# Moving chunk 1's transposes of x from TensorE to the DMA, with a new sequence of turns, in a gated linear attention and MLP kernel

## Chip, cores and metric

One core of one Trainium2 chip runs the whole kernel in one launch. The metric is the device time in microseconds (us) of the execution, median of several runs.

## What is computed

The input is q, k, v and alpha of 4 batches, 8 heads, 768 steps and 48 channels a head. The attention part is a recurrence, and a normalised two-layer MLP with a residual follows it. The reference, cut to what matters:

```python
for t in range(S):
    state = alpha[:, :, t, :, None] * state + einsum('bhd,bhe->bhde', k[:, :, t], v[:, :, t])
    y[:, :, t] = einsum('bhd,bhde->bhe', q[:, :, t], state)
x = y.transpose(0, 2, 1, 3).reshape(B, S, H * D)              # 4 x 768 x 384
mu, var = mean(x), mean((x - mu) ** 2)                        # over the 384 channels
xn = (x - mu) / sqrt(var + 1e-06) * g_ln
out = x + maximum(xn @ w_ch1, 0.0) @ w_ch2                    # 384 -> 1536 -> 384
```

The MLP's weights arrive as 64-bit floating-point words and are turned into 32-bit ones on the chip.

## The kernel before

The 768 steps are cut into six chunks of 128. For each chunk and batch (24 pairs) a generator `attention(c, b)` takes the logarithm of alpha (L285), sums it along the chunk with a triangular matrix on TensorE (L290 for chunk 0, L501 later), scales q and k with its exponentials (L295, L296, L304), turns them (for chunks 0 and 1 with TensorE, L320, and copies to qT and kT, L325 and L327; later through DRAM with a transposing transfer, L335 to L342), forms the scores `aps` (L354, L517), the state's update `ups` (L384) and the output `yps` (L408 for chunk 0, L424 later). ScalarE and VectorE then evict x with its sum (L438 to L445), write it out for the residual (L452), compute the variance (L459 to L462) and the normalised xn (L465 or L469).

The MLP needs x with channels on the partitions. There are two ways for that. For chunks below `X_BY_DMA`, TensorE transposes three 128x128 blocks of xn for each batch (L476), and VectorE copies the result into `xT` (L479 for chunk 0, L482 for others). For the later chunks, xn is split into the two 16-bit halves of each word (`parts`, L485), written to DRAM (`sentx`, L488) and read back with a transposing transfer (L490). The engine of the copy at L485 follows from `PARTED`: GpSimd for chunks below it, ScalarE from it on.

```python
def part(c):
    return nc.gpsimd.tensor_copy if c < PARTED else nc.scalar.copy
...
if c < X_BY_DMA:
    xps = ps.tile([P, NF, P], FP32, name="xps", tag="bank", bufs=8)
    ...
else:
    parts = work.tile([P, 2, DM], UINT16, name="parts", tag="row", bufs=ROWS)
    part(c)(out=parts, in_=xn.bitcast(UINT16).rearrange("t (d w) -> t w d", w=2))
    ...
    nc.sync.dma_start(sent, parts)
    ...
    nc.sync.dma_start_transpose(xT_of[c][:, :, b].bitcast(UINT16),
                                sent.rearrange("t w d -> (t w) d"))
```

The weights come in twelve pieces, named A to L in the sequence, first and second layer in turn. Each is loaded (L191), rounded on VectorE and ScalarE (L201 to L212), and later split into a top and a low part (L226 to L232). The hidden products `hps` (L603) come in groups of 128 hidden channels. For chunk 0 the first ten groups of hidden channels are plain: three products against xT, for two batches at a time where the channel group is one of the first six, else for four. All other groups are "halved": nine products of top, mixed and low parts of weights and x (x split at L554 on ScalarE and L557 on VectorE). The hidden values are evicted as `htop` (L615, ScalarE), `hlow` (L623) and `hmixed` (L632, VectorE); the second layer `ops` (L645) accumulates 384 output channels for each batch, and L664 and L665 add x and store.

Every engine works through its own queue in order, and all transfers but one small one are issued from SP's queue. What stands in these queues, and in which order, is set by the string `ORDER`: each of its characters names a generator (0, 1, 2 the loads of alpha, k and q; 3 those of v; a to x the 24 attention pairs; A to L the weight pieces; M the hidden products, R, N and V their evictions, Y the second layer, X the split of x, Q the results, and so on), and the kernel advances that generator by one step.

```python
with tc.manual_schedule():
    for turn in ORDER:
        next(turns[turn], None)
```

Of the kernel before, what the change touches and what calls it, by code (L numbers as in the profile page):

```python
# [17 lines left out]

EPS = 1e-6
BY_DMA = 2  # L20
X_BY_DMA = 2
STAGED = 3
ROWS = 8
SUMS = 19
# [1 line left out]
TAIL = 3  # L26
KEPT = 2
SPLIT = 6
PARTED = 2
PLAIN = 10  # L30
ROUND_BY_POOL = False
K = 4096.0

ORDER = (
    "000aabc210b21aaaab0dc221b1Aabaadbbbefbaca3acdBc4bddccbcbdcdddAfcaaAbAaAa1eBaaba2"
    "eb3fdCbfabfbBdfbbc0ceBfeeeedf1gdb2BaChCcBcCdd5c34dCMdegMeddMhcgdghhRRRgcg3gfEfhA"
    "cMehfeRec0ChcfeEfhgc5efeeeEYEdgfYeXDgf3fBjfM2RMMhMhFgDD1iRADR4FFRihEYjF3YDhXYjFD"
    "DYFjjXhgjiHMghRjhhhihi0iHigYGYHXYgjgMMgIiAjGkGGijRYRYiHXHXIX1XIIBlMMRR5jKGff43Yl"
    "flkiMKej0KK2R3h0MhKMJIRC1XRKjjejCkFYknjliJ1fUehY2llgJJj0jhehmjkfjgjgkhGYfLi4kiMU"
    "2LLmkmil0lMLRNgLRVjgLgYlTlYYTXXNkiYkXXVXXXiUi3YIUi35onXQXMUplkkQklQlkmRNMiQln0kk"  # L40
    "VlkiiT34knkl2kllRlnnMT1lmONUVRYEjiJN0nYYYmVYETYkpUpMMnnUmmpmlmRGNVk2noIYURNjjkjY"
    "VYYMHHTRll5NV2jmYMnUipniRU13kNpUYnVnqYlYM3iokJnl1pRlnNYmVYo1nTMMUnronooRNRVYYM0N"
    "Vn2UlUUpkRMTYpY4ooUNVXOnXoRNVmYpX0mXUqnnqmmXXmXmXX33mY5npYqorpY3mQqoqqQpoMOrprMs"
    "ORtorNRMVo0qprrNroQropoMoUppRQpRppYYVYYpNYrqq1NVVYM5nY1qmYrRqpqmmNqUp4VYttU2YtM0"
    "qt1pRNUrMoRmOooVNptUUtuYYqoq2YqqMRnnqUoVNVYmsro2Yt3sssssYMRmsMRrUUqqNrVNYYvrqrrr"
    "MMposs1XUVrXrtRNVRYNXXYYXXtVXXXq3YYOY5Qsss4tvMqQvvO0ruuOR2UsUNvQtMsrRtNssssvsuuu"
    "VM0VrtUY1uRssNY3YusrVYYUUvu1YssMvMvQR3qtNRVrYNYtvwxtVttMRYtYu4sNUxUUU5YtVUYuwvrv"
    "vtt22ttwxUMxRutwtNUMVRNYvYYxxvxU3VYMwwxMRNxwYOxVRNVwYYYXMwXMRXNwYXRVNYYVXXXYuOQu"
    "Xvv5XuvwxwwwMRxxx3wuwuNwVMRNuVwOxYYYYUUvwQuuuuMwwvMQRNVRvvvNYMVYYYuOOxRUuNVUYxxY"
    "MxxxRNMYVwUYRwxUvNYQVYxMMRwxxvRONVNYVYYYXXXXXUUMRMUUUNYRXVNVYUMRYNXXYVYYXMQUOMRR"  # L50
    "NYVYNVYYQMRNMYRVYNVYYUUMMRUNVYYRONVMRUNQVOYOOOUYYUYUUMRNMRYMMRNNVVVMRRNVYYYQNVYY"
    "YYQQQQ"
)


# [1 line left out]
def kernel(  # L57
# [212 lines left out]
    def part(c):  # L270
        return nc.gpsimd.tensor_copy if c < PARTED else nc.scalar.copy

# [3 lines left out]
    def attention(c, b):  # L276
# [194 lines left out]
        if c not in xT_of:  # L471
            xT_of[c] = work.tile([P, NF, B, P], FP32, name="xT", tag="xT", bufs=1)
        if c < X_BY_DMA:
            xps = ps.tile([P, NF, P], FP32, name="xps", tag="bank", bufs=8)
# [231 lines left out]
```

## Time and profile before

| | |
|---|---|
| median of 3 runs | 412.56 us (411.27 to 415.81) |
| the profiled execution | 412.15 us |
| its span, first to last instruction | 410.4 us |
| granted TensorE clock, mean | 0.996 |
| busy: TensorE, VectorE, ScalarE, GpSimd | 399.1, 258.3, 221.1, 112.4 us |
| moved by DMA | 66.81 MB |

In the profile, PE is TensorE's products and PEld its loading of weights, DVE is VectorE, ACT is ScalarE, POOL is GpSimd and SPq is SP's queue, which issues transfers. A row of the timeline has the start and the length in us, engine, line, operation, output and inputs, and in square brackets the idle time ahead of it with what ended it. A row of the chain has start, length and the work that the end of the program hangs on there.

### The profile page before, as it was taken

To read this page: it belongs to the slowest core of one execution; us is meant where nothing else is said; L and a number is where in the kernel's file an instruction comes from. 1 tells how busy PE (TensorE), PEld (TensorE's weight loads), DVE (VectorE), ACT (ScalarE), POOL (GpSimd) and SP (SyncE) were. 2 spreads that over 40 slices of the span, in tenths; PEclk is the share of its full clock that TensorE was granted. 3 is DMA by queue.
4 is the path that set the end of the run, shared out by engine and by line. 5 is a ranking of instruction groups with operands and counts; after the bars stand their busy time and mean duration, and the time that the engine had idled before them with its cause. 6 is when DMAs were issued, how large, how long until landed. Compare 5 with 4: busy or idle time off the path is not lost.

```text
span 410.4 us, 10816 instructions
## 1 busy us (share of the span) xinstructions
PE 399.1 (97%) x4418; PEld 334.9 (82%) x4418; DVE 258.3 (63%) x424; ACT 221.1 (54%) x489; POOL 112.4 (27%) x122
## 2 busy tenths in 40 slices
PE   8779999999999999999999999999999999999996
PEld 6668777646789888889888879879989889889886
DVE  4699898989987755775444774463573346443262
ACT  5688687479749674563675648355328443111120
POOL 4224301002145435121243325351041084130000
PEclk9989999999999999999999999999999999999999
DMA  6985996994848769968367958867435032010302
GB/s 193 308 260 150 276 282 193 276 279 159 191 117 256 200 162 207 207 167 247 87 176 193 218 151 250 176 142 195 107 61 173 23 102 53 21 58 2 96 19 77
DMA packets 103562, 66.81 MB, mean 163 GB/s; under 512 B 70444, under 2 KB 95532, under 8 KB 103512
## 3 DMA queue, kind: packets, MB, share of 16 engines
q1 hardware_dynamic: 103480, 66.12, 59.5%
q8 instruction: 34, 0.56, 0.6%
q14 instruction: 16, 0.13, 0.1%
q0 software_dynamic: 32, 0.00, 0.0%
HBM read 34.29 MB, written 20.28 MB: 133 GB/s over the span
## 4 chain that ended last, share of the span: by engine, by line
PE 92%; DMA 3%; ACT 2%; SPq 1%; DVE 1%; issue 1%; ACTq 0%
PE hps L603 39%; PE ops L645 39%; PE yps L424 5%; PE ups L384 3%; PE aps L517 3%; DMA vn<-in_v_dram 2%; PE lps L501 2%; DMA ra<-in_alpha_dram 1%; PE yps L408 1%; PE tps L320 1%; SPq L125 1%; PE xps L476 1%; DVE hmixed L632 1%; ACT xn L459 0%; SPq L129 0%
## 5 line engine op out<-in xcount | busy, mean ns | idle before, releaser
L615 ACT ACTIVATE htop<-hps 128x512 fp32r<-128x512 f32 (+2 forms) x78 | 43.9, 564 | 120.3 <-PE hps L603 116.3
L623 DVE SCALAR_TENSOR_TENSOR hlow<-hps,htop 128x512 fp32r<-128x512 f32 x62 | 42.8, 690 | 90.9 <-ACT htop L615 88.3
L569 POOL TENSOR_TENSOR wmixed<-top,low 128x384 fp32r<-128x384 f32 x62 | 70.1, 1140 | 96.1 <-PE hps L603 41.0
L645 PE MATMUL ops<-top,htop 128*128 128x384 f32 x248 | 56.7, 344 | 0.0
L645 PE MATMUL ops<-low,hmixed 128*128 128x384 f32 x248 | 55.3, 339 | 0.0
L603 PE MATMUL hps<-xtop,top 128*128 128x512 f32 x186 | 54.5, 401 | 0.0
L603 PE MATMUL hps<-xmixed,low 128*128 128x512 f32 x186 | 53.4, 395 | 0.0
L645 PE MATMUL ops<-ws,hlow 128*128 128x384 f32 x240 | 53.4, 338 | 0.0
L603 PE MATMUL hps<-xlow,wmixed 128*128 128x512 f32 x186 | 53.4, 395 | 0.0
L632 DVE SCALAR_TENSOR_TENSOR hmixed<-hlow,htop 128x512 fp32r<-128x512 f32 x62 | 48.0, 779 | 3.2
L645 PEld LDWEIGHTS ops<-top,htop 128*128 128x128 f32 x248 | 44.1, 188 | 3.7 <-ACT xn L469 0.6
L645 PEld LDWEIGHTS ops<-low,hmixed 128*128 128x128 f32 x248 | 44.3, 188 | 0.8 <-DVE hmixed L632 0.3
L645 PEld LDWEIGHTS ops<-ws,hlow 128*128 128x128 f32 x240 | 43.0, 188 | 0.0
L603 PEld LDWEIGHTS hps<-xmixed,low 128*128 128x128 f32 x186 | 35.0, 188 | 8.4
L603 PEld LDWEIGHTS hps<-xlow,wmixed 128*128 128x128 f32 x186 | 34.9, 188 | 8.2
L603 PEld LDWEIGHTS hps<-xtop,top 128*128 128x128 f32 x186 | 33.6, 188 | 6.7 <-DVE mid L392 0.6
L394 POOL TENSOR_TENSOR mid<-mid,gate 112x192 f32<-112x192 f32 x20 | 13.4, 672 | 86.5 <-DVE mid L392 51.9
L335 ACT COPY planes<-qk 128x1024 uint16<-128x1024 uint16 x32 | 32.7, 1039 | 1.5 <-DVE qk L304 1.5
L394 POOL TENSOR_TENSOR st<-st,gate 112x192 f32<-112x192 f32 x16 | 16.1, 1005 | 53.5 <-DVE st L392 51.1
L645 PE MATMUL ops<-w,htop 128*128 128x384 f32 x80 | 27.8, 493 | 0.0
L603 PE MATMUL hps<-xT,w 128*128 128x256 f32 (+1 forms) x96 | 27.1, 433 | 0.0
L603 PEld LDWEIGHTS hps<-xT,w 128*128 128x128 f32 x96 | 18.1, 190 | 8.3 <-issue 5.1
(121 smaller groups left out, 662.2 us busy)
## 6 DMA issues: line engine op xcount, KB each, us to landing
ws<-in_moe_w_ch_dram SPq DMA_DIRECT2D x12, 768.0 KB
sent<-planes SPq DMA_DIRECT2D x32, 256.0 KB
vn<-in_v_dram SPq DMA_DIRECT2D x12, 384.0 KB
kept<-x SPq DMA_DIRECT2D x20, 192.0 KB
rq<-in_q_dram SPq DMA_DIRECT2D x16, 192.0 KB
rk<-in_k_dram SPq DMA_DIRECT2D x16, 192.0 KB
ob<-kept SPq DMA_DIRECT2D x16, 192.0 KB
sentx<-parts SPq DMA_DIRECT2D x16, 192.0 KB
```

The lines of the kernel that those rows point to most:

```text
L335: part(c)(out=planes, in_=natural.rearrange("t (d w) -> t w d", w=2))
L384: nc.tensor.matmul(up[h, p], qk_of(c, b)[1][ts, p, i, :h.stop - h.start], vn[ts, i, p], start=True, stop=True)
L394: nc.gpsimd.tensor_mul(new, new, gate[:R, s].unsqueeze(2).broadcast_to([R, NP, D]))
L424: nc.tensor.matmul(yps[r][halves[s], i, p], of, by, start=not (odd and inner), stop=bool(inner or not odd), skip_group_check=bool(odd))
L501: nc.tensor.matmul(lps[halves[h ^ i ^ 1], :DM], tri[halves[h], halves[h]], las[c, b + i][halves[h]], start=True, stop=True)
L517: nc.tensor.matmul(aps[halves[i ^ n], p, s], kT[rs, p, s], qT[rs, p, s], start=True, stop=True)
L569: nc.gpsimd.tensor_add(mixed_of[g], *(first_weights(w, g[1]).bitcast(FP32) for w in (top_of, low_of)))
L603: nc.tensor.matmul(hps, ws[n][:, f], xs[f][n][:, cs], start=(n == f == 0), stop=(n == len(ws) - 1 and f == NF - 1))
L615: nc.scalar.activation(out=t, in_=hps, func=AFT.Relu, scale=1.0 if g in halved else K ** -2)
L623: nc.vector.scalar_tensor_tensor(out=t, in0=hps, scalar=0.0, in1=top.bitcast(FP32), op0=AOP.max, op1=AOP.subtract)
L632: nc.vector.scalar_tensor_tensor(out=t, in0=low.bitcast(FP32), scalar=1 - K, in1=top.bitcast(FP32), op0=AOP.mult, op1=AOP.add)
L645: nc.tensor.matmul(acc_of[c, b], hidden_of[g][n + 1][:, (b - bs[0]) * P:][:, :P], by, start=(j == n == 0), stop=last)
```

## The change

`X_BY_DMA` goes from 2 to 1, so chunk 1's x takes the way of the split halves and the transposing transfer; only chunk 0 is still transposed on TensorE. `PARTED` goes from 2 to 1; with both, the copy at L485 of chunk 1 is ScalarE's. `ORDER` is replaced by another string; both are cut here to their first three lines and the last.

```diff
 BY_DMA = 2
-X_BY_DMA = 2
+X_BY_DMA = 1
 STAGED = 3
...
-PARTED = 2
+PARTED = 1
...
 ORDER = (
-    "000aabc210b21aaaab0dc221b1Aabaadbbbefbaca3acdBc4bddccbcbdcdddAfcaaAbAaAa1eBaaba2"
-    "eb3fdCbfabfbBdfbbc0ceBfeeeedf1gdb2BaChCcBcCdd5c34dCMdegMeddMhcgdghhRRRgcg3gfEfhA"
-    "cMehfeRec0ChcfeEfhgc5efeeeEYEdgfYeXDgf3fBjfM2RMMhMhFgDD1iRADR4FFRihEYjF3YDhXYjFD"
...
-    "YYQQQQ"
+    "000aa2bbcca12130ba2aacbaabbbAbaaaadab1cbbbbAc1adbc2abdc0a0Babaabdcda1bbdAdcedda2"
+    "fAbhbcgdA44deCBM3ffecRfBMfRBffcedegCefeec3BC1dc5hdC2dCdge3heeBcddhceMdRMccgffhhd"
+    "RhhAfcgfAgdge0gfCEEce5eghYEYiefEe1cgf3CEjMRDfM2FDRfFDfDM3RMMXFg4iejFYYgRiFgYYefh"
...
+    "NVYYYQQQYQ"
 )
```

More of the change, by code (lines that the diff above doesn't have):

```diff
@@ L34 @@
 ORDER = (
-    "000aabc210b21aaaab0dc221b1Aabaadbbbefbaca3acdBc4bddccbcbdcdddAfcaaAbAaAa1eBaaba2"
-    "eb3fdCbfabfbBdfbbc0ceBfeeeedf1gdb2BaChCcBcCdd5c34dCMdegMeddMhcgdghhRRRgcg3gfEfhA"
-    "cMehfeRec0ChcfeEfhgc5efeeeEYEdgfYeXDgf3fBjfM2RMMhMhFgDD1iRADR4FFRihEYjF3YDhXYjFD"
-    "DYFjjXhgjiHMghRjhhhihi0iHigYGYHXYgjgMMgIiAjGkGGijRYRYiHXHXIX1XIIBlMMRR5jKGff43Yl"
-    "flkiMKej0KK2R3h0MhKMJIRC1XRKjjejCkFYknjliJ1fUehY2llgJJj0jhehmjkfjgjgkhGYfLi4kiMU"
-    "2LLmkmil0lMLRNgLRVjgLgYlTlYYTXXNkiYkXXVXXXiUi3YIUi35onXQXMUplkkQklQlkmRNMiQln0kk"
@@ L41 @@
[L41 to L51, printed above, removed]
-    "YYQQQQ"
+    "000aa2bbcca12130ba2aacbaabbbAbaaaadab1cbbbbAc1adbc2abdc0a0Babaabdcda1bbdAdcedda2"
@@ new lines @@
+    "fAbhbcgdA44deCBM3ffecRfBMfRBffcedegCefeec3BC1dc5hdC2dCdge3heeBcddhceMdRMccgffhhd"
+    "RhhAfcgfAgdge0gfCEEce5eghYEYiefEe1cgf3CEjMRDfM2FDRfFDfDM3RMMXFg4iejFYYgRiFgYYefh"
+    "hHjjRhXffgYhYgHgjgefDgiI0iYHEHGHXMMR1RiXkGXXGiiYYjlMGhhKRhjYhghjGj4IKMMXCh3KRIeY"
+    "lKEIRhXKlJhhYXMMigjgIgKJieJJgRf52RLUe3fjMjhilhLFLgejfYjUGLA0lYRlkUkhlMk0NjLjLTkl"
+    "kkYTVXiXkXjllkXjjkYRi1NVYiXmjiYXXU3QiinXiUiB4XDQ5nm1MBTUkRk3MQlljjljNROmkj22lknM"
+    "kkVlN0IQ3kiniUVlknkYnRnDiNnYTkmUG0mmH2iYYVMYYmRNYijF3VYnpl3ol4jJlMllHmTMRlNRYnVN"
@@ new lines @@
+    "lp1mV3lYYIJ2k0TYlUmoMppkRj115NUVYY0mnnnUinlopppnoMmoRNnViUnTrnpYqnk0YopoUkmo1MpR"
+    "mnkNVoMmYoRmUUYmm2kmN4V5q0lpYrYqoToornOXprM2XrR3sXqMNVo1omq2RNYXqrr1YYorXVXXq3Xr"
+    "oXqYotUonop4QUpstrq2MUnRNQOqMppto3ppVnppoRN3MtYoYYpVYo0nUQMmUmRmRmnONVNYUvQo1YY5"
+    "ttMqrVrrnoYrRUMtspstUNRVsN1YrppVYYYsttMrspqRsNY0rrrrq0qMpVRuqqYsqqqsOO2UmN425Vss"
+    "YtmuuvYsvuMMUspuu3uRRvU0tuNYVNVYYY2Xv1MvMvXXRN2VXXXRwUUNsYUVUvqvXYYYqqqtXXqvMuRQ"
+    "QtttutNMVO1xttRtstQ4sNss5vvutuxu33vxMUrvRwYYYVttxNVxUYMwxrRrNVYsOsY3YYMRxMqNVYRY"
@@ L53 @@
+    "tUtNVssutUUUMrrRNVwwvwYrxYQssYwwYMMRNVquYYsURNYxVYuuvvrXXuwwMXUMRNVRYNMvYUxVXXXX"
+    "RYYONXO5XxUVvvxxvwwxwwxYMRNYQwxxQwxwvYwxwUUOVYwMRvwMRxNVNVUuuuYwYYYUMMRNRVNVYYYY"
+    "MxwUxRNwUMUUVYYvvxURNYOuVYQxMMuOURRxNYVUNYUYVYMMuXXXRNVYYRMNXXXVYXXRNVYXYYQMOQMR"
+    "RNVNYYVYQYOQUUMMORONYVRYNUVMRNYVYYYUUMRNMVRNVOOYQYYYUUUUUMMRNRYMVMMNVRYYYORRNVNV"
+    "NVYYYQQQYQ"
 )
```

## The prediction

> **What bounds the kernel now.** I read the page's first parts, then the busy time by stage, then the chain that ended last in order of time.
>
> ```profile
> span 410.4 us, 10816 instructions
> PE 399.1 (97%) x4418; PEld 334.9 (82%) x4418; DVE 258.3 (63%) x424; ACT 221.1 (54%) x489; POOL 112.4 (27%) x122
> ...
> GB/s 193 308 260 150 276 282 193 276 279 159 191 117 256 200 162 207 207 167 247 87 176 193 218 151 250 176 142 195 107 61 173 23 102 53 21 58 2 96 19 77
> ```
>
> ```profile
> 0.00:20.00 20.00, 15.79 (x138) 12.07 (x139) 10.93 (x31) 12.14 (x26) 6.75 (x18) 0.99 0.78 248
> 20.00:40.00 20.00, 17.73 (x307) 15.47 (x304) 18.18 (x32) 17.36 (x47) 6.75 (x6) 0.93 0.71 215
> 40.00:60.00 20.00, 19.41 (x387) 15.37 (x386) 18.14 (x32) 15.03 (x36) 4.02 (x5) 1.00 0.93 267
> 80.00:100.00 20.00, 20.00 (x185) 11.06 (x174) 18.41 (x30) 17.11 (x41) 3.57 (x4) 1.00 0.76 241
> 240.00:280.00 40.00, 39.23 (x415) 33.23 (x414) 22.02 (x38) 24.51 (x54) 16.48 (x16) 1.00 0.74 179
> 360.00:410.40 50.40, 46.95 (x238) 42.53 (x236) 19.00 (x30) 6.59 (x11) 3.92 (x3) 1.00 0.14 49
> ```
>
> The columns after the length are PE, PEld, DVE, ACT and POOL busy, then granted clock, DMA share and GB/s. TensorE bounds the kernel: 11.3 us of it are idle, of which the first 60 us hold 7.1 (4.21, 2.27 and 0.59), the stage from 240 holds 0.77, and the end 3.45. VectorE is the second engine: above 18 us of 20 in the three later early stages shown. So a change can gain at the start, where TensorE has holes, or by taking work off TensorE; later only the order's small losses are left.
>
> The first 35 us are worse than the busy column says. On the chain and among TensorE's and VectorE's instructions:
>
> ```profile
> 11.37 7.47 DMA vn<-in_v_dram
> ...
> 34.91 4.08 PE hps L603 x18
> ...
> 47.84 2.78 PE ops L645 x8
> 50.61 5.18 PE hps L603 x24
> ```
>
> ```profile
> 7.83 0.56 DVE L304 TENSOR_TENSOR qk<-rq,eq 128x384 f32<-128x384 f32 x1 [0.28 <-DMA rq<-in_q_dram]
> ...
> 8.97 0.69 DVE L325 COPY kT<-tps 112x512 f32<-112x512 f32 x1
> ...
> 17.72 0.56 DVE L201 TENSOR_SCALAR w<-ws 128x768 int32<-128x768 int32 x1 [1.04 <-DMA ws<-in_moe_w_ch_dram]
> ...
> 20.94 0.96 DVE L209 SCALAR_TENSOR_TENSOR ws<-ws 128x768 int32<-128x768 int32 x1 [0.80 <-ACT ws L207]
> ...
> 35.63 0.94 DVE L212 TENSOR_TENSOR w<-w,ws 128x768 f32<-128x768 f32 x1
> ...
> 46.31 1.15 DVE L212 TENSOR_TENSOR w<-w,ws 128x768 f32<-128x768 f32 x1
> ```
>
> The steady stream of hidden products (hps, L603) starts at 34.9 us. Ahead of it TensorE waits for v, then for the chain of statistics behind v, while VectorE rounds weights (L201 to L212). The first weight piece (letter A) waits for its transfer until 17.72; the second hidden piece (C) is rounded by 36.57, and the third (E) by 47.46. The stream of four plain groups at 50.61 uses E.
>
> **The change, part by part.**
>
> *Transposes taken off.* Twelve of the 24 transposes at L476 go (three for each batch of chunk 1), and the four copies at L482.
>
> ```profile
> 82.51 7.72 PE hps L603 x18
> ...
> 94.69 0.48 PE xps L476 x3
> 97.75 0.66 PE xps L476 x6
> 106.65 0.33 PE xps L476 x3
> ```
>
> ```profile
> L482 DVE COPY xT<-xps x4: 551/553/559, 97.2 to 107.7; 128x384 f32<-128x384 f32 x4
> L485 ACT COPY parts<-xn x16: 815/828/834, 138.9 to 332.6; 128x768 uint16<-128x768 uint16 x16
> L488 SPq DMA_DIRECT2D sentx<-parts x16: 332/400/607, 140.5 to 334.9; - x16
> L490 SPq DMA_TRANSPOSE xT<-sentx x16: 1215/1252/1565, 143.2 to 338.4; - x16
> ```
>
> On the chain the twelve cost 0.48 + 0.66 + 0.33 = 1.47 us, and TensorE is what the chain runs through there: minus 1.5. VectorE loses 4 x 0.55 = 2.2 us, in the stage where it is fullest; I count that at nothing by itself, since it only keeps VectorE from catching up with TensorE.
>
> *Added.* Four copies on ScalarE (4 x 0.83 = 3.3 us), four writes and four transposing transfers on SP's queue (4 x 0.40 + 4 x 1.25 = 6.6 us of issue). PARTED falls with X_BY_DMA, so the copy of chunk 1 is ScalarE's, as it was for chunks 2 to 5. All this I cost at nothing if the cover holds: ScalarE is busy 17.11 of 20 in the stage from 80, so 2.9 us stand free there, and more in front of it. For the transfers the cover is the TensorE work between the first such copy and the first product of chunk 1. The built order has there one run of six plain 512-wide products, eight plain second-layer ones, two halved groups of nine, 24 second-layer products, and attention: by counts and the chain's rows (7.72/18 = 0.43 us a pass of a plain one, two passes each, and below 2.1 for nine or twelve of the others) about 25 us. What must fit is bounded by chunk 2 of today: first copy at 138.9, last transpose issued at 159.72.
>
> ```profile
> 159.72 1.25 SPq L490 DMA_TRANSPOSE xT<-sentx  x1
> ...
> 166.46 0.71 ACT L554 ACTIVATE xtop<-xT,small 128x512 fp32r<-128x512 f32 x1
> 168.02 0.60 ACT L615 ACTIVATE htop<-hps 128x512 fp32r<-128x512 f32 x1 [0.84 <-PE hps L603]
> ```
>
> That is 22 us to the last issue, or 27.6 to the first use, with the four copies spread over 12 us by the order; the new order has them within seven instructions of ScalarE, so I estimate 16 to 20 us and a free margin of 5.
>
> The Trainium skill, page "VectorE: DVE Perf Modes", section "Rules for kernel authors", speaks against the change: it sends a 128x128 transpose to TensorE where PSUM can take it and to the DMA only otherwise, and its section "The three transpose paths" gives, for one of 16-bit elements, 390 ns against 1309. The rows here agree in size (0.11 to 0.16 us for one on the chain, 1.25 us to issue three), but the dearer path is paid on another engine; by the rule alone the four batches would cost some 5 us instead of saving 1.5.
>
> *The new sequence at the start.* v of batches 0 and 1 moves from the 18th issue on SP's queue to the 8th, weight piece A from the 17th to the 13th. Today the seventh load (196.6 KB each, so 1.38 MB) has landed at 7.83 by the L304 row; v adds 0.39 MB, at the 193 to 308 GB/s of the first two slices 1.3 to 2.0 us: v lands near 9.4 instead of 18.84. It then no longer bounds; TensorE's wait for it goes. Piece A now stands behind two small writes that wait for ScalarE's exponentials, whose ends today let it go near 7.65 (estimate):
>
> ```profile
> 6.80 0.48 ACT L295 ACTIVATE eq<-lps 128x384 f32<-128x384 f32 x1
> ...
> 10.89 0.43 SPq L191 DMA_DIRECT2D ws<-in_moe_w_ch_dram  x1
> ```
>
> Issued at 10.89 it was used at 17.72, 6.83 us later; the same again gives 14.5, so VectorE starts on A 3.2 us earlier. But three L304 (0.56) and two kT copies (0.69) that stood ahead of A now stand behind it; started every 0.47 and 0.6 us they are about 2.7 us, and by E's end the built order has 3.9 us more there. So C is rounded by 36.57 - 3.2 + 2.7 = 36.1, less what VectorE saves of its waits on the way (today 17.9 us between these ends hold 15.6 us of instructions, and 0.80 of the rest is the wait shown): 33.8 to 36.1. E: 47.46 - 3.2 + 3.9 = 48.2, less 0 to 4.1 (29.7 us that hold 25.6): 44.1 to 48.2. The third plain group starts today about 37.6 (two groups of six passes into the run of 18), a microsecond after C; in the new order it can only start with C, so 1.5 to 3.8 us earlier. From there to the run at 50.61 the new order has about 0.5 us less TensorE work, so that run comes 2.0 to 4.3 us earlier; E allows it. I take 3.1, the middle.
>
> *Half-clock stretch.* The 0.93 in the stage from 20 is 1.4 us of lost clock:
>
> ```profile
> 18.98 1.38 PE L384 MATMUL ups<-vn,qk 128*64 128x48 f32 x31 [1.82 <-DMA vn<-in_v_dram]
> ...
> 20.19 3.30 PE L408 MATMUL yps<-vn,at 128*64 128x48 f32 x63
> ...
> 30.83 1.11 PE L408 MATMUL yps<-vn,at 128*64 128x48 f32 x31
> ```
>
> 63 products took 3.30 us where 31 later took 1.11. It follows TensorE's idle 1.82 ahead of v. The new order moves that idle to between 15 and 24 us rather than removing it: I take nothing, with minus 1.4 to plus 1.4 as bounds. The Trainium skill, "TensorE: Matmul & The Clock Gate", section "Part 1: The HAM clock gate", has a free-running window of about 3.4 us, after an idle one of which the clock is halved; by it one such window is lost again, which leaves the sum as it is.
>
> *Changes of shape on TensorE.* After a block of attention products on part of the array, the first full-array block is longer:
>
> ```profile
> 111.67 1.08 PE yps L424 x64
> 112.75 2.32 PE ops L645 x12
> ...
> 161.67 2.11 PE ops L645 x12
> ...
> 391.57 6.26 PE hps L603 x27
> 397.83 9.14 PE ops L645 x52
> ```
>
> 2.32 against 2.11: 0.2 us a change. The built order has 38 such changes against 32: plus 1.2. The last blocks (27 and 52) are the same in both orders: nothing at the end.
>
> *Sum.* Against the profiled execution, 412.15 us (span 410.4 and 1.75 around it): 412.15 - 1.5 - 3.1 + 1.2 = 408.75. Of the two single holes left (0.59 and 0.77) an order that avoids gaps may close about a quarter, 0.35: 408.4. The profiled run is 0.41 below the median of 412.56; I don't carry that.
>
> **The rivals.**
>
> *The head start is given back* (VectorE). It is over 90% busy from 20 to 100 us, and every product needs weights rounded and x split there. If its pace and not TensorE's queue sets the early stage, the 3.1 are lost and only 1.5 - 1.2 remain: about 411.8. For it: C's and E's steps carry 2.7 to 3.9 us more. Against: TensorE's busy 20.00 in the stage from 80 shows that VectorE kept up, and it loses 2.2 us.
>
> *More is closed than I count.* The upper ends together: 4.3 at the start, the half-clock stretch gone (1.4), both holes (1.36) gone: 412.15 - 1.5 - 4.3 + 1.2 - 1.4 - 1.36 = 404.8. For it: in the built order the rounded weights stand further ahead of their use. Against: weights by DMA set the pace at 0.93 of all engines from 40 to 60.
>
> *x of chunk 1 comes late (slower).* ScalarE works in order; its three xtop (L554) of chunk 1 wait for the fourth transpose, and behind them stand the eviction of the last group of chunk 0 and chunk 2's logarithms. It decides from the point where the last transpose lands more than about 20 us after the first copy. If the chain is as long as today's for chunk 2, 27.6 and three steps of about 1 us against 25, TensorE waits 5.2; with the 6.6 us of SP issue passed on to the loads of chunk 2 as well, 11.8. Middle 8.5: 408.4 + 8.5 = 416.9. For it: DMA share 0.76 there, and SP issues in order. Against: the margin of 5.
>
> *The change doesn't do what it says* only in PARTED: the copy stays on ScalarE, as costed.
>
> **How the numbers follow.** About 1%, 4.1 us, is what a measurement of this kernel can tell from no change: faster is below 408.4, slower above 416.7. Forecast 0.46, its own range 406 to 411, rather more than half of it faster by the margin (0.28); more closed 0.14, faster; given back 0.20, within; late x 0.20, of which 0.15 slower. Sum: faster 0.42, within 0.42 (0.18 + 0.20 + 0.04), slower 0.16 with what lies beyond the cases. The range goes from 404.5, the lower rival, to 415.5, which takes in the smaller half of the late x.
>
> **What would show it.** Right: v used before 12 us; the first L201 near 14.5; the first hps near 24 and the third near 35; TensorE busy 20 of 20 from 60 on; no xps after 60 us; a granted clock below 1 once in the first 30 us. Wrong: a wait of ScalarE's xtop on xT of over 3 us or of TensorE's first chunk 1 group (late x); the third hps at 37 or later (given back); more than 1 us of TensorE idle in any stage after 110 us, for which I have no term.

## The result, and the profile after

The changed kernel took 420.19 us (median of 4 runs, 418.31 to 425.83) against 414.19 us for the kernel before, run beside it: a ratio of 1.0129, with a 95% interval from 1.0084 to 1.0173; the ratio leaves out the run of 425.83 us, whose granted clock was 0.980 against 0.986 to 0.995 in the other three. Run again later it had 1.0208 (1.0172 to 1.0244). It is slower by 1.3 to 2.1%. The forecast was 408.4 us, and the range ended at 415.5. The profiled execution took 420.57 us, 8.42 more than the one of before. The page:

```profile
span 418.9 us, 10812 instructions
...
PE 403.0 (96%) x4406; PEld 336.1 (80%) x4406; DVE 259.2 (62%) x420; ACT 224.5 (54%) x493; POOL 105.5 (25%) x122
...
PE 90%; DMA 4%; DVE 2%; ACT 1%; issue 1%; SPq 1%; DVEq 0%
```

The twelve transposes are gone (x4406 for x4418), yet TensorE is busy 3.9 us longer, and idle 15.9 us (418.9 - 403.0) in place of 11.3 (410.4 - 399.1). The chain now holds 4% of DMA; it had none behind the loads of the start. The stages, with TensorE's busy time second, and the granted clock and DMA share third and second from the end:

```profile
0.00:20.00 20.00, 17.17 (x186) 13.59 (x186) 11.47 (x33) 14.77 (x36) 6.74 (x18) 1.00 0.76 231
20.00:40.00 20.00, 16.00 (x280) 13.02 (x279) 17.70 (x30) 14.96 (x38) 5.94 (x7) 1.00 0.96 290
40.00:60.00 20.00, 19.73 (x333) 15.28 (x333) 17.42 (x31) 12.94 (x30) 2.67 (x5) 1.00 0.63 177
...
100.00:120.00 20.00, 17.21 (x283) 13.20 (x282) 18.26 (x27) 11.66 (x23) 7.67 (x8) 0.98 0.93 212
120.00:140.00 20.00, 19.78 (x268) 17.29 (x267) 15.19 (x23) 15.28 (x34) 5.15 (x5) 0.94 0.66 197
160.00:180.00 20.00, 18.41 (x267) 15.47 (x260) 9.64 (x18) 8.07 (x19) 5.04 (x6) 0.91 1.00 194
```

Two of these stages before:

```profile
100.00:120.00 20.00, 20.00 (x300) 15.38 (x299) 17.91 (x29) 14.03 (x31) 5.54 (x6) 1.00 0.65 162
160.00:180.00 20.00, 20.00 (x309) 17.18 (x308) 15.24 (x26) 10.75 (x25) 5.69 (x6) 1.00 0.77 183
```

The new waits lie behind 100 us; in the first 60 us TensorE is idle 7.1 us in both. From 100 to 120 us 2.79 us are idle and from 160 to 180 us 1.59. The granted clock (0.98, 0.94, 0.91) takes 3.4 us more: the trace has two stretches of 3.41 us at half the clock, at 119.12 and 173.73 us, where the kernel before has one, at 19.49. So the 8.5 us of span are 4.6 of idle time, 1.7 of lost clock, and 2.2 of TensorE's own work. The chain names what was waited for (start, length, work):

```profile
32.87 1.78 issue
...
50.26 6.67 PE hps L603 x30
...
112.96 4.19 DMA turned<-sent
...
169.16 3.91 DMA turned<-sent
...
224.72 4.74 DMA turned<-sent
```

And TensorE's waits, as total, number and longest:

```profile
PE aps L517 <- DMA turned<-sent: 4.6, 3, 2.8
```

A transfer's length on the chain goes on from its issue to its landing; TensorE's three waits are 2.79, 1.59 and 0.2 us of it. `turned` is not x. It is q and k of chunks 2, 3 and 4, turned by DMA as they were before; each time it is the second pair of batches, and the score products (L517) wait. So TensorE does not wait for x of chunk 1: something else is late because of it, or because of the new sequence. The experiments had to tell which.

### The profile page after: what moved, and what is told of

It is laid out like the page before. It is cut to its first block, busy times and chain, and to the rows that moved or that the text cites. A ratio compares the mean times of both kernels' runs of the same rounds, so it can differ in the third digit from the quotient of the medians.

```text
span 418.9 us, 10812 instructions
## 1 busy us (share of the span) xinstructions
PE 403.0 (96%) x4406; PEld 336.1 (80%) x4406; DVE 259.2 (62%) x420; ACT 224.5 (54%) x493; POOL 105.5 (25%) x122
## 4 chain that ended last, share of the span: by engine, by line
PE 90%; DMA 4%; DVE 2%; ACT 1%; issue 1%; SPq 1%; DVEq 0%
PE ops L645 38%; PE hps L603 37%; PE yps L424 4%; DMA turned<-sent 3%; PE ups L384 3%; PE aps L517 3%; PE lps L501 1%; DMA rk<-in_k_dram 1%; PE aps L354 1%; PE tps L320 1%; PE yps L408 1%; DVE qk L304 1%; SPq L125 1%; DVE hmixed L632 1%; ACT kT L325 0%
## 5 line engine op out<-in xcount | busy, mean ns | idle before, releaser
L569 POOL TENSOR_TENSOR wmixed<-top,low 128x384 fp32r<-128x384 f32 x62 | 68.9, 1121 | 105.6 <-PE hps L603 61.6
L603 PE MATMUL hps<-xtop,top 128*128 128x512 f32 x186 | 55.6, 407 | 0.0
L632 DVE SCALAR_TENSOR_TENSOR hmixed<-hlow,htop 128x512 fp32r<-128x512 f32 x62 | 50.1, 808 | 4.1 <-DVE hlow L623 0.5
L603 PEld LDWEIGHTS hps<-xmixed,low 128*128 128x128 f32 x186 | 35.5, 191 | 8.6
L603 PEld LDWEIGHTS hps<-xlow,wmixed 128*128 128x128 f32 x186 | 35.3, 190 | 8.2
L394 POOL TENSOR_TENSOR mid<-mid,gate 112x192 f32<-112x192 f32 x20 | 12.1, 610 | 73.8 <-DVE mid L392 72.6
L394 POOL TENSOR_TENSOR st<-st,gate 112x192 f32<-112x192 f32 x16 | 13.1, 821 | 66.1 <-DVE st L392 66.1
L603 PEld LDWEIGHTS hps<-xT,w 128*128 128x128 f32 x96 | 17.9, 190 | 8.5 <-issue 5.4
```

What stands on the lines that cost most here:

```text
L394: nc.gpsimd.tensor_mul(new, new, gate[:R, s].unsqueeze(2).broadcast_to([R, NP, D]))
L569: nc.gpsimd.tensor_add(mixed_of[g], *(first_weights(w, g[1]).bitcast(FP32) for w in (top_of, low_of)))
L603: nc.tensor.matmul(hps, ws[n][:, f], xs[f][n][:, cs], start=(n == f == 0), stop=(n == len(ws) - 1 and f == NF - 1))
L632: nc.vector.scalar_tensor_tensor(out=t, in0=low.bitcast(FP32), scalar=1 - K, in1=top.bitcast(FP32), op0=AOP.mult, op1=AOP.add)
```

## Where the queue stands: the transposes that TensorE waits for

The first of the three waits, in the timeline of before. ScalarE's last copy of q and k, SyncE's four transposing transfers behind it, and TensorE's products:

```profile
103.09 1.03 ACT L335 COPY planes<-qk 128x1024 uint16<-128x1024 uint16 x1
...
104.60 5.70 SPq L342 DMA_TRANSPOSE turned<-sent  x4
...
115.00 1.16 PE L517 MATMUL aps<-turned 48*64 48x64 f32 x64
```

The same after:

```profile
96.47 4.67 SPq L490 DMA_TRANSPOSE xT<-sentx  x3
...
102.29 1.99 ACT L335 COPY planes<-qk 128x1024 uint16<-128x1024 uint16 x2
...
102.34 1.25 SPq L490 DMA_TRANSPOSE xT<-sentx  x1
...
104.25 1.38 SPq L129 DMA_DIRECT2D ra<-in_alpha_dram  x2
105.73 1.00 SPq L338 DMA_DIRECT2D sent<-planes  x2
...
106.23 1.34 ACT L554 ACTIVATE xtop<-xT,small 128x512 fp32r<-128x512 f32 x2 [1.95 <-issue]
...
107.32 0.81 SPq L338 DMA_DIRECT2D sent<-planes  x1
108.23 5.98 SPq L342 DMA_TRANSPOSE turned<-sent  x4
...
117.29 1.28 PE L517 MATMUL aps<-turned 48*64 48x64 f32 x64 [2.79 <-DMA turned<-sent]
```

Before, the copies end at 104.12 and the transposes are issued 0.48 us later. After, the copies end at 104.28 and the transposes begin 3.95 us later: SyncE spends 5.92 us on issuing chunk 1's x from 96.47 on, and the writes and loads that came up meanwhile are served one after another until 108. TensorE needs the result at about the same time in both (115.00 and, with the wait taken off, 114.5). Before, that was met without a wait, and with a small margin: the products start 4.7 us behind the end of the last issue (110.30), and where they had to wait it was 2.3 to 4.0 us (3.1 here, the ends in e3 and e5 below). So the margin was some 1 to 2 us, an estimate from these, against a delay of 3.5.

## The experiments

All ratios are to the kernel before, run beside each.

| run | what it is | ratio | 95% interval |
|---|---|---|---|
| e9 | the changed kernel again | 1.0208 | 1.0172 to 1.0244 |
| e1 | new sequence, x by TensorE | 1.0225 | 1.0174 to 1.0275 |
| e2 | old sequence, x by DMA | 1.0306 | 1.0237 to 1.0375 |
| e10 | new to turn 262, then old | 0.998 | 0.9937 to 1.0023 |
| e12 | new to turn 170, then old | 0.9973 | 0.9938 to 1.0009 |
| e11 | old to turn 262, then new, x by DMA | 1.0185 | 1.012 to 1.025 |
| e16 | new to turn 440, x by DMA, then old | 1.0157 | 1.0088 to 1.0225 |
| e3 | before + 8 unread transfers | 1.0213 | 1.0143 to 1.0282 |
| e7 | the same, 4 of them plain | 1.0127 | 1.0073 to 1.018 |
| e15 | 8 unread ones at chunk 5 | 1.0172 | 1.012 to 1.0223 |
| e17 | 8 unread ones behind all else | 0.9968 | 0.9931 to 1.0005 |
| e13 | changed, 8 transfers taken out | 1.0063 | 1.003 to 1.0096 |
| e5 | changed, the 8 on ScalarE's queue | 1.0145 | 1.0065 to 1.0226 |
| e18 | changed, alpha loads by GpSimd | 1.0022 | 0.9984 to 1.006 |
| e4 | changed, three score turns later | 1.012 | 1.0057 to 1.0184 |
| e8 | e4 mended | 1.0172 | 1.0103 to 1.0241 |
| e14 | e13 and e8 together | 1.023 | 1.0177 to 1.0283 |
| e6 | changed, three loads later | 1.0174 | 1.0118 to 1.0229 |

The changed kernel's own two ratios differ by 0.8%, so smaller differences between runs that were not on a chip together are not read; e4, e5, e6 and e8 are not told apart from it by their times, only by their traces. In e4 the next chunk's batch overwrites q and k of two batches before they are used, and in e13 and e14 chunk 1's x stays untransposed: these three don't compute the reference, and stand here for their times alone.

**Sequence or path.** e1 is the new sequence with `X_BY_DMA = 2`:

```diff
-X_BY_DMA = 1
+X_BY_DMA = 2
```

> The new sequence with chunk 1's x still transposed on TensorE (X_BY_DMA = 2): four copies, four writes and four transposing transfers fewer than the changed kernel, 12 transposes (1.5 us) more. Theory O (the new sequence itself places the second pairs' score products of chunks 2 to 4 too close behind their transposed q and k, whatever chunk 1's path): the three waits of aps at 113, 169 and 225 us stay at 3 us or more each, 417 to 421 us. Theory L (the four writes and four transposing transfers, 12 us of all the DMA engines' time and 6.6 us of SyncE's queue, push the other transposes back): at least the first wait goes, the others shrink below 2 us, 407 to 413 us.

It took 424.02 us, and neither theory had it right: none of the three waits is over 1 us, yet the time is as long. TensorE waits elsewhere:

```profile
100.51 1.50 PE L517 MATMUL aps<-turned 48*64 48x64 f32 x62 [2.01 <-DVE xT L482]
```

Here the scores wait, not for their inputs, but for VectorE's copy of x out of the buffers that TensorE writes. The sequence was made for the other path, and the copy stands late in it. So e1 doesn't isolate the sequence. e2 is the reverse:

```diff
-X_BY_DMA = 2
+X_BY_DMA = 1
-PARTED = 2
+PARTED = 1
 # the last letter of e, f, g and h doubled (one step more on this path)
```

> The old sequence with chunk 1's x by DMA (X_BY_DMA = 1, PARTED = 1; the last letter of each of chunk 1's four attentions doubled, since this path has one step more). Theory O: the waits of aps on the transposed q and k do not come; what is lost is a direct wait for x of chunk 1, since the old sequence leaves ScalarE's xtop only a few instructions behind the last copy: 5 to 9 us of TensorE idle once near 100 us, 416 to 421 us. Theory L: beside that the aps waits of 3 us or more also appear after 110 us, 422 us or more.

428.62 us. No wait for q and k came. TensorE stood still twice, 4.71 us at 105 and 4.83 us at 120, and the chain has chunk 1's x behind both:

```profile
98.69 4.87 DMA sentx<-parts
...
116.39 2.84 DMA sentx<-parts
...
119.25 3.17 DMA xT<-sentx
```

The first is ScalarE's next copy (103.59 us on the chain), held up by a write of x; the second is x itself. This is the prediction's third rival, on the old sequence, and twice rather than once. Two sequences can be joined instead: the first n turns of one, then the other with the turns already taken left out.

> The first 262 turns of the new sequence (to about 60 us), then the old sequence with the turns already taken left out; chunk 1's x on TensorE as before. If the start gains the 3.1 us that the prediction put there: 409 to 411.5 us. If, as the changed kernel's trace has it, the run of plain products at 50 us comes only 0.35 us earlier: 412 to 416 us, within 1% of the kernel before. A wait for transposed q and k near 115 us is expected by neither.

> As the run with the new start, but only the first 170 turns (to about 38 us), up to which the new sequence has v early, weight piece A early and C rounded by 34.8 us. If the gain is made there and lost again between 38 and 60 us: 409 to 412 us. If there is none to be had: 412 to 416 us.

> The first 262 turns of the old sequence, then the new sequence with the turns already taken left out; chunk 1's x by DMA. Theory O+L (the loss is made after 60 us, by the transfers and by where the new sequence puts its score products): 418 to 424 us, with aps waiting 2.5 us or more near 115 us. If the new start is at fault (its DMA share of 0.96 from 20 to 40 us, its waits inside small products): 412 to 415 us.

e10 and e12 have the time of before, e11 the loss, with waits for `turned` of 1.81, 1.21, 1.89 and 1.50 us at 117, 153, 174 and 232 us. The loss is made behind the 262nd turn, near 60 us. e9 is the changed kernel again, as the measure for these:

> The changed kernel itself once more, as the measure for the runs beside it on the same chip: 418 to 421 us, a wait of aps for the transposed q and k of 2.5 us or more near 115 us, and a granted clock below 0.95 from 120 to 140 us.

424.35 us; the wait near 117 us was 3.08 us, and the clock from 120 to 140 us 0.88.

**Number or place of the transfers.** e3 adds the eight transfers to the kernel before and nothing reads them:

```diff
             for f in range(NF):
                 nc.tensor.transpose(xps[:, f], xn[:, f * P:(f + 1) * P], ident)
+            if not whole:
+                sent = dram.tile([P, 2, DM], UINT16, name="sentx", ...)
+                nc.sync.dma_start(sent, xn.bitcast(UINT16)...)
             yield
...
                 nc.vector.tensor_copy(out=xT_of[c][:, :, b], in_=xps)
+                junk = work.tile([P, NF, P], FP32, name="junk", ...)
+                nc.sync.dma_start_transpose(junk.bitcast(UINT16), sent...)
```

> The kernel before, plus the four writes of chunk 1's normalised x (196 KB each) and the four transposing transfers, whose result nothing reads; chunk 1's x still comes from TensorE. Theory L: 416 us or more, with waits of aps on the transposed q and k of 3 us or more after 105 us. Theory O: the old sequence has room for them, within 2 us of the kernel before (411 to 415 us), no aps wait over 1 us.

423.10 us, with the whole loss in one wait. SyncE's rows and the products:

```profile
109.16 0.38 SPq L479 DMA_DIRECT2D sentx<-xn  x1
...
112.24 1.23 SPq L487 DMA_TRANSPOSE junk<-sentx  x1
113.52 5.77 SPq L342 DMA_TRANSPOSE turned<-sent  x4
...
121.57 2.11 PE L523 MATMUL aps<-turned 48*64 48x64 f32 x64 [5.22 <-DMA turned<-sent]
```

By its time this would fit theory L, the load on the DMA engines. The rows say something narrower: SyncE takes its issues in order, and between 109.54 and 112.24 it stands still until the unread write has landed, with the wanted transposes behind it. They go out 8.9 us later than before (113.52 for 104.60). e7 makes the four reads plain ones:

> The run with the load alone on the old sequence, but its four unread transposing transfers are plain ones of the same bytes (196 KB), from the same queue at the same places. Theory T (the price lies in the transposing form: 1.25 us of issue and packets of 256 bytes): the wait of aps of 5.2 us at 116 to 121 us falls below 1 us, 413 to 416 us. Theory B (any four more transfers at that place do it): 3 us or more stay, 420 us or more.

420.18 us, the wait still 3.29 us; the transposing form is not the price, or only a part of it. SyncE stands still here too, from 107.53 to 110.43 us, until the unread write has landed. e15 puts the eight at chunk 5, where the DMA share is low:

> The kernel before with four unread writes and four unread transposing transfers, of the same size as in the run with the load alone, but at chunk 5's x, from 320 to 340 us, where the DMA share is 0.34 and not 0.65 to 0.75. Theory L (the price is the delay of the transfers that TensorE waits for just behind): no price here, within 1% of the kernel before, 412 to 416 us. If the transfers cost by their number, wherever they stand: 420 us or more.

423.05 us, against theory L: again each unread transpose waits for its own write in front of one of chunk 5's real ones, and ScalarE's xtop waits 8.25 us for x. e17 has the same eight once more, the reads behind the last transfer that is waited for, and the writes long landed by then:

```diff
             nc.sync.dma_start(kept, x)
+            if c == 5:
+                nc.sync.dma_start(more, x.bitcast(UINT16)...)
...
             nc.sync.dma_start_transpose(xT_of[c][:, :, b].bitcast(UINT16), sent...)
+            for more in more_of.values() if (c, b) == (5, 1) else ():
+                nc.sync.dma_start_transpose(junk.bitcast(UINT16), more...)
```

> The kernel before with the same four unread writes and four unread transposing transfers once more, now placed so that none of them stands on SyncE's queue ahead of a transfer that is waited for: the writes with chunk 5's x kept, the transposes behind the last of chunk 5's own (from 340 us). Theory S (the price of the eight is what stands behind them on SyncE's in-order queue, 5 us of transposes' issue and any wait for their own writes): within 1% of the kernel before, 412 to 417 us, and xtop's wait for x near 341 us about 1.4 us as before. If eight more transfers cost by their number or bytes: 420 us or more.

```profile
339.95 2.54 SPq L494 DMA_TRANSPOSE xT<-sentx  x2
342.58 5.23 SPq L498 DMA_TRANSPOSE junk<-more  x4
```

0.9968: the eight cost nothing. In the old sequence it is their place on the queue that costs, with the wait for their own write that they bring to it, and not their number or bytes. (The place differs in load too, 0.31 of the DMA engines' time from 320 to 340 us; but e15 had that place as well and paid.)

**In the changed kernel.** e13 takes the eight out of it:

```diff
-            nc.sync.dma_start(sent, parts)
+            if c > 1:
+                nc.sync.dma_start(sent, parts)
             yield
+            if c == 1:
+                nc.gpsimd.tensor_copy(xT_of[c][:, :, b], xn...)
```

> The changed kernel without chunk 1's four writes and four transposing transfers: GpSimd copies x untransposed into the same tile in their place (four copies of some 1 us on an engine that is 25% busy), so chunk 1's second-layer inputs are not the reference's; instructions, order and all else stay. Theory L (the eight transfers on the DMA engines make the transposed q and k late): the wait of aps near 115 us goes under 0.5 us, with the low clock behind it, 411 to 416 us. Theory O (the new sequence's rest is too tight in itself): the wait near 115 us or its followers near 155, 175 and 230 us keep 3 us or more together, 418 to 424 us.

1.0063. The first wait is gone, and the clock is full (timeline, then stages):

```profile
105.23 1.98 ACT L335 COPY planes<-qk 128x1024 uint16<-128x1024 uint16 x2
...
107.92 5.96 SPq L342 DMA_TRANSPOSE turned<-sent  x4
```

```profile
100.00:120.00 20.00, 20.00 (x324) 15.31 (x323) 18.54 (x29) 14.38 (x27) 8.16 (x10) 1.00 0.69 164
120.00:140.00 20.00, 19.61 (x270) 17.16 (x270) 17.02 (x26) 16.30 (x36) 4.47 (x7) 1.00 0.77 215
```

The transposes go 0.71 us behind the last copy. TensorE is 3 us later at this place than in the changed kernel's trace (the run of 30 products starts at 53.3 us for 50.2), so the distances are to be compared and not the times. The idle time is not less: from 100 to 280 us TensorE is idle 5.7 us in this trace and 4.9 in the changed kernel's. What the trace has gained there is the clock, 3.4 us. What remains of the loss, 0.6%, is the sequence's own: this run still waits 0.89, 1.91 and 0.77 us for `turned` at 153, 175 and 230 us. e5 moves the eight to ScalarE's queue:

```diff
-            nc.sync.dma_start(sent, parts)
+            queue = nc.scalar if c == 1 else nc.sync
+            queue.dma_start(sent, parts)
```

> The changed kernel with chunk 1's four writes and four transposing transfers issued from ScalarE's queue in place of SyncE's. Theory Q (SyncE's queue: in the changed kernel it issues without a pause from 96.5 to 114.3 us, and the second pair's transposes stand behind 5.9 us of x transposes): the wait of aps for the transposed q and k at 113 us falls from 2.8 us to under 0.5, TensorE's clock of 0.94 behind it goes, 413 to 417 us. Theory E (the DMA engines' own time: 0.93 of all engines from 100 to 120 us): the wait stays above 2 us and ScalarE pays for the issue, 419 to 424 us.

421.35 us, the wait as long:

```profile
98.07 1.31 ACTq L491 DMA_TRANSPOSE xT<-sentx  x1
...
102.25 1.22 ACTq L491 DMA_TRANSPOSE xT<-sentx  x1
...
106.74 1.98 ACT L335 COPY planes<-qk 128x1024 uint16<-128x1024 uint16 x2
...
110.10 5.48 SPq L342 DMA_TRANSPOSE turned<-sent  x4
...
119.53 1.53 PE L518 MATMUL aps<-turned 48*64 48x64 f32 x64 [2.82 <-DMA turned<-sent]
```

SyncE is free now and issues 1.4 us behind the last copy, but that copy comes 4.4 us later (108.72 for 104.28), since ScalarE issues x's transposes ahead of it. The delay has changed its queue. The Trainium skill, page "DMA: Bandwidth & Descriptors", section "Issuing engines are not separate DMA queues", says that starting transfers on several engines saves only the sequencer's time, "which is usually small relative to the DMA itself". Here that time is not small: 5.23 us to issue four transposes in a row (e17's last row), against 2.9 to 5.3 us from issue to landing of one in the changed kernel. e18 takes other issues off SyncE, to an engine that has time:

```diff
+                    queue = nc.gpsimd if n == "a" and c > 2 else nc.sync
...
-                        nc.sync.dma_start(
+                        queue.dma_start(
```

> The changed kernel with the alpha loads of chunks 3 to 5 issued from GpSimd's queue (25% busy) and not SyncE's; 1.95 us of them stand today ahead of the late transposes. Theory S: those transposes issue about 2 us sooner after the last copy of q and k (today 3.9 us after it), the wait of aps near 117 us falls from 3 us to about 1, 1 to 4 us below the changed kernel's ratio, 416 to 420 us. If the DMA engines' time sets it: the wait stays at 2.5 us or more. If GpSimd's own waits for free buffers come into it: later, with waits of wmixed or mid on GpSimd.

1.0022: most of the loss is gone, with all of chunk 1's transfers in place (its ten runs go from 413.11 to 422.20 us). The DMA engines are no less busy than in the changed kernel, 1.03 of their time from 100 to 120 us for 0.93, so their load isn't the price.

```profile
108.15 6.06 SPq L343 DMA_TRANSPOSE turned<-sent  x4
...
116.52 1.43 PE L518 MATMUL aps<-turned 48*64 48x64 f32 x64 [1.07 <-DVE first L665]
```

The wait is 1.07 us and no longer one for the transposes. But they are issued only 0.6 us sooner behind the last copy (108.15 for 104.76) than in the changed kernel, not the 2 us expected: in the time won, SyncE waits 1.0 us for the write to land. And a wait of 2.29 us for `turned` now stands at 227 us, where the changed kernel had 0.2. As in e13, the trace has its gain in the clock: full from 100 to 360 us. So what stands on SyncE's queue is shown as the lever, while the way from there to the whole 1 to 2% is not followed.

**Moving the scores.** If the products come too early, they can come later. e4 and e8 put 4 to 5 us of other products ahead of three score turns. e8's edit:

```diff
-5nm1MBTUkRk3M ... 5q0lpYrYqoToornOXprM ... 5VssYtmuuvYsvuM
+nm1MBTUR3M5kk ... q0lYYqTnOXM5prooorpr ... VYmuuYuM5sstvsv
```

> The changed kernel with three of its score turns (second pairs of chunks 2, 3 and 4) and the same pair's next steps moved behind 4 to 5 us of hidden and output products. Both theories: if the three stalls are the loss, they go (together 12.8 us on the chain, with the low clock of 0.94 and 0.91 behind the first two worth some 3 us): 405 to 410 us, with the run of 30 plain products still at 50 us. If the waits only move on to whatever comes behind, because TensorE is ahead of the transfers everywhere: 416 us or more.

> The run with three score turns later, again, with the next chunk's batch 1 kept behind the moved products (in the run before it overwrote q and k of two batches too early). Theory M (in the new sequence TensorE is fed just in time all through 100 to 190 us, so the wait moves on to whatever comes next): waits for transposed q and k under 1 us together, others (ups on VectorE's at, ops on hlow) 2 us or more in their place, 417 to 421 us. If the three waits were the whole loss: 408 to 413 us.

418.93 and 422.63 us. In e8 no wait of 0.4 us for `turned` is left, and the time is that of the changed kernel:

```profile
119.02 1.39 PE L384 MATMUL ups<-vn,qk 64*64 64x48 f32 x36 [0.83 <-DVE at L368]
...
177.07 0.97 PE L603 MATMUL hps<-xtop,top 128*128 128x512 f32 x3 [0.72 <-DVE qk L304]
...
228.25 0.98 PE L645 MATMUL ops<-low,hmixed 128*128 128x384 f32 x4 [1.12 <-DVE hmixed L632]
```

The waits have moved to what stands behind: `ups` waits for VectorE's `at`, which now follows the scores at once. TensorE's idle time from 100 to 280 us is 6.3 us, more than the changed kernel's 4.9. e14 does it without the transfers:

> As the run without the transfers, with the three score turns moved later as well. If load and places of the scores are the whole loss: 407 to 412 us, below the kernel before. If TensorE in the new sequence is fed just in time from 100 to 240 us by VectorE and ScalarE too: waits of ups on at and of ops on hlow or hmixed as in the run with the scores later, 414 to 421 us.

1.023, slower than e13 alone, and no faster than e8 (1.0172), which has the transfers. So with the scores moved, taking the transfers out gives nothing back. This fits theory M (fed just in time, so that a wait moved is not a wait saved); it is not shown beyond that. e16 asks where behind turn 440 the loss is made:

> The new sequence with chunk 1's x by DMA up to its 440th turn (just ahead of the scores whose transposed q and k are late near 115 us), then the old sequence with the turns already taken left out. If one wait near 115 us with the low clock behind it is most of the loss: 418 us or more. If the later waits (155 to 235 us) of the new rest make half of it: 415 to 418 us, with one wait near 115 us and none of 1 us behind it up to 240 us.

```profile
114.83 0.29 PE L517 MATMUL aps<-turned 48*64 48x64 f32 x2 [2.46 <-DMA turned<-sent]
119.47 1.98 PE L517 MATMUL aps<-turned 48*64 48x64 f32 x62 [4.35 <-ACT x L438]
```

1.0157, all of it here, with no wait of 1 us behind it until 258 us. The 4.35 us come from the joint itself (the second score buffer waits for ScalarE's x), so the run shows that the old rest adds nothing, but not what the one wait is worth in the new.

**The unnamed waits at the start.** e6 moves three loads behind the scores of chunk 1's second pair:

```diff
-eYEYiefEe1cgf3CEjMRDfM2FDRfFDfDM3RMMXFg4iej
+eYEYiefEecgfCEjMRDfMFDRfFDfDM3RMMXFg4132iej
```

> The changed kernel with three of chunk 2's loads (k of two batches, v of two, q of two, 0.4 MB each) moved some 20 turns later, just ahead of chunk 2's first exponential. Theory I (TensorE's unnamed waits inside blocks of small products, 1.78 us at 32.9 in the changed kernel and 3.45 and 2.89 at 43 to 47 in two others with the same start, are its own instructions coming late: the transfer of 16 KB of them that ends about 1.3 us before TensorE goes on stands among 4.4 MB of loads): with 1.2 MB less ahead of it the wait at 43 to 47 us stays under 1 us, the DMA share from 40 to 60 us rises, and the time is 1 to 3 us below the changed kernel's. If it is not that: a wait of 1.5 us or more stays between 30 and 47 us, and the time within 1 us or later.

421.89 us; the wait, 2.34 us at 43.4, stayed. Theory I is not confirmed by this. What the traces have for it stands in the last section.

## Why the prediction was wrong, step by step

*What bounds the kernel: right.* TensorE is 96% busy, and the loss is TensorE's.

*The transposes taken off, minus 1.5: right as far as it shows.* No xps stands on the chain behind 43.45 us. The rows set beside the quoted 390 and 1309 ns do not agree with them in size, as it says: 0.11 to 0.16 us is a third of the one, and 1.25 us issues three of the other.

*The added transfers at nothing: this step failed.* It asked only whether x would reach its first use, and there it was right: ScalarE takes up x 16.7 us after the first copy begins (106.23 against 89.55 us), inside the 16 to 20 forecast. ScalarE stands idle 1.95 us ahead of it, under the 3 us of the sign, and TensorE does not wait for it. It did not ask what stands behind the eight on the same queue. The 6.6 us of issue were written down and then dropped, in the rival too, where they were passed on to chunk 2's loads and not to its transposes. Behind them stood transposes that TensorE took up at 115.00 us with a margin of 1 to 2 us. They are issued 3.5 us later behind the copies that they turn (3.95 for 0.48); TensorE waits 2.79 to 3.08 us, and its clock costs 1.7 to 3.4 us more (one stretch at half the clock, and two in e9). That is 4.5 to 6.5 us at this place for a term of 0. Taking the eight out (e13) gives 0.7 to 1.5% of the whole back, 3 to 6 us; the lower end is within the difference between the changed kernel's own two measurements, and with the scores moved (e14 against e8) it gives nothing. So the wait and its place are shown, and the whole price is not.

*The new start, minus 3.1: right in part.* v is used at 10.51 us and C is rounded at 34.8, as forecast; E is rounded at 49.6, 1.4 us behind the forecast's end. (Its sums of VectorE's waits don't come out of the trace of before: from 17.72 us on, VectorE is busy 16.96 of 18.85 us to C's end and 26.39 of 29.74 to E's, and not 15.6 of 17.9 and 25.6 of 29.7.) The third plain group starts at 37.8 us, which is the prediction's sign of a head start given back; in e9, e10 and e13 it starts at 35.3 to 35.5, as forecast. The run of plain products should have come 2.0 to 4.3 us sooner than 50.61. In three of the twelve traces that have all 262 turns of this start it did:

```profile
47.45 6.74 PE L603 MATMUL hps<-xT,w 128*128 128x256 f32 x30
...
72.61 2.99 PE L645 MATMUL ops<-w,htop 128*128 128x384 f32 x6 [2.32 <-ACT htop L615]
```

These rows are e10's; e14 and e16 have 47.84 and 47.77. In the other nine, the changed kernel's among them (50.19), an unnamed wait of 1.0 to 3.5 us inside the scores of chunk 1 stands ahead of it, and the run comes at 48.4 to 53.3. So the gain came where this wait did not, and the sum has no term for the wait. In e10 the second row, a wait at the joint of the two sequences, gives most of the gain back.

*The shape changes, plus 1.2: too small, or something is missing beside them.* TensorE's busy time less the lost clock is 399.6 us (403.0 - 3.4) for 397.4 (399.1 - 1.7): 2.2 more, where minus 1.5 and plus 1.2 make 0.3 less. No run measures what the other 2.5 us are.

*The single holes, minus 0.35:* the one from 40 to 60 us shrank from 0.59 to 0.27 and the one behind 240 us went; two larger ones came.

*The rivals.* The late x had the right sign, and its time, 416.9 us, was the nearest; that is partly luck, since its place was wrong: not ScalarE's xtop but the next pair's scores. (Its 5.2 us are 5.6 by its own terms, 27.6 + 3 - 25.) "More than 1 us of TensorE idle in any stage after 110 us, for which I have no term" is the sign that came true.

*The rest of the loss.* About 0.6% is left without the transfers (e13), although the transposes' 1.5 us are saved in it too. It is made by the new sequence between 140 and 260 us; the waits of e13 show where, and e14, which should have removed them, only moved them. What would remove them stays open. No version here beats the kernel before by more than the measurement tells.

## What to carry to other kernels

An added transfer costs at least two things: its own way, and what stands behind it on the queue that issues it. Before calling it hidden, list the next transfers on that queue that some engine takes up with little margin, and add the issue time (some 1.3 us for each transposing one here) and any wait for a preceding write. In this kernel, issuing the added transfers from another busy engine moved the delay (e5), and issuing other loads from an engine with time to spare removed most of the loss (e18).

## What was not expected of the hardware

In the nine executions of the new start that have one, TensorE's unnamed wait comes at one of two places: after the 597th recorded product (13 products into the scores of chunk 1's second pair) or the 343rd, 254 earlier. In e1, from 42.67 to 46.12 us:

```profile
46.12 1.44 PE L517 MATMUL aps<-qT,kT 48*64 48x64 f32 x51 [3.45 <-issue]
```

In just that stretch the transfers hold one packet of the queue for instructions:

```profile
q8 instruction: 1, 0.02, 2.0%
```

The whole run has 34 of them, 0.56 MB, so 16 KB each. The Trainium skill, page "Runtime: NRT & Kernel Launch", section "Instruction fetch mechanics", says that an engine's instructions are refilled in blocks of 16 KiB by a DMA queue of its own, and that crossing a block is "mostly hidden". The size agrees with the trace. "Hidden" does not, if these waits are that: 1.0 to 3.5 us in nine of twelve executions, while the DMA engines are 0.88 to 0.98 busy from 20 to 40 us. In all nine, such a packet ends 1.3 to 1.7 us before TensorE goes on. In the three executions without the wait, the packet that belongs to the 597th product starts at 40.2 to 40.3 us; in the six that wait there, at 41.4 to 44.3. So a late packet and the wait go together. That the loads make it late is not shown: e6, with fewer of them in front, still had 2.34 us.

A longer wait does not always cost more clock: 1.59 us at 173 went with a clock of 0.91 over 20 us, 2.34 us at 45 in e6 with 1.00. The Trainium skill, page "TensorE: Matmul & The Clock Gate", section "Part 1: The HAM clock gate", has a free-running window, which would fit both.
